# Regrouping the transfers on one DMA queue of a fused attention and MLP kernel

## The chip, the cores and the metric

The kernel runs on one core of a Trainium2 chip. The metric is the device time of one execution in microseconds. Five executions of the kernel before the change took 925.91 to 928.11, with a median of 926.62.

## The reference, cut to what matters

```python
def _attn_ref(q, k, v, g_norm):                 # q, k, v: (8 batches, 8 heads, 576, 64) float32
    kv = np.einsum('bhsd,bhse->bhde', k, v)
    out = np.einsum('bhsd,bhde->bhse', q, kv)
    rms = np.sqrt(np.mean(out * out, axis=-1, keepdims=True) + 1e-06)
    return (out / rms * g_norm)

def _moe_ref(x, w_in, w_out):                   # x: (4608, 512), w_in: (512, 2048), w_out: (2048, 512)
    h = x @ w_in
    sp = np.maximum(h, 0.0) + np.log1p(np.exp(-np.abs(h)))
    g = h * erf(sp)
    return g @ w_out

x = attn_out.transpose(0, 2, 1, 3).reshape(4608, 512)    # the bridge between the two
```

Attention is linear, so each head needs k^T v (64 x 64), q times that, and a normalisation. Its result feeds an MLP whose two weight matrices come as float64. The kernel reads them as pairs of 32-bit words and converts them itself.

## The kernel before the change

**Groups and periods.** The 4608 tokens are worked on in nine groups of 512: one for the first 512 tokens of each batch, and a ninth made of the last 64 tokens of all eight. While one group goes through the MLP, the attention of the next one is computed beside it, two heads (a pair) at a time, four pairs to a group. The hidden features are handled in 16 tiles of 128.

- Head (L729 to L758): the attention of group 0, and the first loads.
- First loop (L822 to L928), groups 0 and 1, one hidden tile in each step n. In group 0 the weights are loaded (load_w, L208) and converted to float32 (w_split, w_join). In group 1 each tile is cut into three parts (w_upper L645 on ACT, w_lower L661 on DVE), so that a product of full precision can be made from three fast ones, and the parts are stored to a scratch area in HBM (L668, L672). ACT cuts into a buffer of four in the pool w_in_p, and has to wait until the store of the tile that had that buffer before has landed.
- Second loop (L976 to L1077), groups 2 to 8. I call one pass a **period** and number it by its m, 8 to 36. In period m PE makes four hidden tiles (hidden, L676: 12 products at L634 each, which read x_forms and w_in_parts), and after them the four results of the period before (result, L950: again 12 products at L634 each, which read g_forms and w_out_parts). In between stand the few matmuls of one attention pair of the next group (visit L428, mean L483).

**What a period loads.** Four tiles of w_in and four of w_out, 768 KB each, come back from the scratch area through load_parts (L765, issued at L773). w_in has four buffers: one comes free when its hidden tile is done, and is needed again at the same place a period later. w_out has seven: all four of a period come free only when PE is through with the last of the four results, since every result reads all four. Three tiles are thus loaded ahead, and the fourth follows in the first buffer that comes free. A period also loads k, v and q of the pair that is two ahead (load_pair L123, load_q L152): k and v as 115 rows of five tokens (L141) and one odd row (L146) each, q in eight small transfers of 32 and 40 KB that bring it in 32 x 32 blocks (L162), which DVE then turns (turn, L314, at L318). k, v and q have two buffers each. At the end of a group (periods 8, 12, 16 and so on) four output tiles are stored (store, L698, at L705).

**What sets the order.** Every engine runs the order in which the program is written. All these transfers are issued by SP, one after the other, so a transfer that has to wait holds up all that are behind it. A transfer also waits for a semaphore: the program gives the transfers of this queue eight semaphores in turn, so one can be issued only when the one that stands eight places ahead of it has landed. That is why the trace shows SP waiting at L162 for "DMA v_sb".

In a period, the calls fetch(place) set the order, with place 0 to 3 after the four hidden tiles and 4 to 7 after the four results, and `loads` stands at place 3:

```python
    FETCH = ("", "in", "in", "out", "in", "out", "in", "out out")
    load_parts("out", BATCH)
```

So SP sees, from one period to the next: w_in, w_in, k, v, q (8 transfers), w_out, w_in, w_out, w_in, w_out, w_out, with the output stores among the last ones. In the steps of groups 0 and 1, k, v and q of a pair are loaded in one go, in the step that has a pair's first products (`loads` after visit).

Of the kernel before, what the change touches and what calls it, by code (L numbers as in the profile page):

```python
# [49 lines left out]

BATCH = 4
LAG = 5


FIRST = 2
WHOLE = 2
SHIFT = 4096.0
SQ = 32
# [3 lines left out]
def kernel(  # L62
# [10 lines left out]
    nc = tc.nc  # L73
    P = 128
    B, H, S, D = q.shape
# [4 lines left out]
    NP = H // 2  # L80
# [30 lines left out]
    exp_ln_table()  # L111


    q_sb, k_sb, v_sb = {}, {}, {}


    q_last = early.tile([P, 2, 2, D], FP32, name="q_last", bufs=1)
# [1 line left out]
    def chunks(T):  # L119

        return 6 if T == 0 else 5

    def load_pair(i, turned=True):  # L123
        T, p = divmod(i, NP)
        if T >= B:
            return
        pool = early if i in (2, 3) else kvp
        side = nc.scalar if i < 3 else nc.sync
        if T == 0:
            t = pool.tile([P, G if pool is early else S], FP32, name="q_sb", tag="q")  # L130
            t = q_sb[T, p] = t[:, 0:G].rearrange("p (j h d) -> p j h d", j=J, h=2)
            nc.sync.dma_start(
                out=t, in_=q[T, 2 * p : 2 * p + 2, 0:G, :].rearrange("h (p j) d -> p j h d", j=J)
            )
        for name, got, src in (("k", k_sb, k), ("v", v_sb, v)):
            C = chunks(T)
            rows, rest = divmod(S, C)
            assert rest < 2
            t = got[T, p] = pool.tile([rows + rest, 2, C, D], FP32, name=f"{name}_sb", tag=name)
            heads = src[T, 2 * p : 2 * p + 2]  # L140
            side.dma_start(  # L141
                out=t[:rows].rearrange("r h c d -> r h (c d)"),
                in_=heads[:, : S - rest].rearrange("h (r c) d -> r h (c d)", c=C),
            )
            if rest:
                side.dma_start(  # L146
                    out=t[rows:, :, 0], in_=heads[:, S - rest :].rearrange("h r d -> r h d")
                )
        if T > 0 and turned:
            load_q(i)  # L150

    def load_q(i):  # L152


        T, p = divmod(i, NP)
        t = q_sb[T, p] = kvp.tile([P, S], FP32, name="q_sb", tag="q")
        for n in range(P // SQ):
            h, w = divmod(n, D // SQ)
            to = t[n * SQ : n * SQ + SQ].rearrange("a (j b) -> a j b", b=SQ)
            for head, js in ((1 - h, slice(0, G // 2 // SQ)), (h, slice(G // 2 // SQ, S // SQ))):  # L160
                src = q[T, 2 * p + head, :, w * SQ : w * SQ + SQ]
                nc.sync.dma_start(  # L162
                    out=to[:, js], in_=src.rearrange("(j a) b -> a j b", a=SQ)[:, js]
                )
# [78 lines left out]
    def w_join(which, f, k):  # L243
# [122 lines left out]
    def attention(T, p, pools=None, in_parts=False):  # L366
# [5 lines left out]
        apart = FIRST < T < B  # L372
# [177 lines left out]
            split_lower()  # L550

        def loads():
            load_pair(T * NP + p + 2)

        if T == 0:
            return products, apply, halve, mean, norm
# [4 lines left out]
        first_ = (partial(prepare, T, p),) if (T, p) == (1, 0) else ()  # L561
        then_ = partial(turn, *then)
        if apart:
            pieces = (first_, (visit, halve, keep_tail), (loads, then_))
            return (*(partial(chain, *group) for group in pieces), mean, norm, *after)
        pieces = (first_, (visit, loads), (halve, keep_tail) if halves else (keep_tail,))
        return (*(partial(chain, *group) for group in pieces), mean, partial(chain, norm, then_), *after)
# [176 lines left out]
    for i in range(NP + 3):  # L744
        for piece, p in ((0, i), (1, i - 1), (4, i - 3), (3, i - 2)):
            if 0 <= p < NP:
                first[p][piece]()
        if i == 1:
            for _ in range(RAW - 2):
                w_next("load")  # L750
            load_pair(NP, turned=False)
            load_pair(NP + 1, turned=False)
        for what in w_rounds.get(i, ()):
            w_next(what)


    w_late.append(True)
    load_q(NP)  # L758
    first_batch, batches = FIRST * NB, NG * NB
    w_seq = {  # L760
        which: [(which, f) for _ in range(NG - FIRST) for f in range(FC)] for which in ("in", "out")
    }
    w_seq["out"][:0] = [("out", f) for f in range(FC - BATCH, FC)]

    def load_parts(which, n):  # L765


        pool = w_out_p if which == "out" and len(w_seq["out"]) > BATCH else w_in_p
        for _ in range(n):
            if w_seq[which]:  # L770
                key = w_seq[which].pop(0)
                t = pool.tile([P, 3, G], FP32, name=f"w_{which}_parts", tag="w")
                nc.sync.dma_start(out=t, in_=w_kept[key])  # L773
                w_now.setdefault(key, []).append(t)
# [47 lines left out]
    for n in range(FIRST * FC + 1):  # L822
        T, f = divmod(n, FC)
        if n == FC:
# [4 lines left out]
            w_in_p = ctx.enter_context(tc.tile_pool(name="w_in_p", bufs=BATCH))  # L829
# [17 lines left out]
        while due(0):  # L847
            weights()
        done = n - LAG + 1
        if T == 0 and done >= 0:  # L850
# [11 lines left out]
        elif T < FIRST:  # L862
# [10 lines left out]
            for i, c in blocks:  # L873
# [4 lines left out]
                    start=(c == 0),  # L878
                    stop=(c == KC - 1),
                )  # L880
        if T < FIRST:
            if n == whole:
                old_h = acc.tile([P, BATCH, G], FP32, name="h", tag="e")
            h = hs[n] = old_h[:, n - whole] if n >= whole else unit("h_sb")
            s = ss[n] = unit("s_sb")
            if n in plain:
                nc.scalar.copy(h, plain.pop(n))
            else:
                nc.scalar.activation(h, n_ps, AF.Copy, scale=SHIFT - 1.0)
# [12 lines left out]
            nc.scalar.activation(s, h, AF.Softplus)  # L902
            if n == 0:
                w_next("split")
            if n == 1:
                load_q(NP + 1)
            for piece in steps[f][1]:
                piece()
            if f % BATCH == BATCH - 1:
                for i in range(n - BATCH + 1, n + 1):  # L910
                    nc.scalar.activation(ss[i], ss[i], AF.Erf)  # L911
                softplus_table()
            if T == FIRST - 1:
# [10 lines left out]
        if T < FIRST:  # L924
            for piece in steps[f][2]:
                piece()
    for n in range(whole, FIRST * FC):
        gates(n)  # L928

# [3 lines left out]
    ctx.enter_context(tc.tile_pool(name="shift_r", bufs=1, side="right")).tile([P, 496], FP32, name="shift_r")  # L933
    late_r = ctx.enter_context(tc.tile_pool(name="late_r", bufs=1, side="right"))
    gate_r = ctx.enter_context(tc.tile_pool(name="gate_r", bufs=1, side="right"))
    w_out_p = ctx.enter_context(tc.tile_pool(name="w_out_p", bufs=7, side="right"))

    def part(h, half):
        return h[:, :, half * 2 * P : half * 2 * P + 2 * P]
# [30 lines left out]
                store(T, j, es[j], cols)  # L970


    FETCH = ("", "in", "in", "out", "in", "out", "in", "out out")
    load_parts("out", BATCH)
    g_next = []
    for m in range(first_batch, batches + 1):  # L976
        T, b = divmod(m, NB)
        todo = []
        last_ = b == NB - 1 and T + 1 < NG
        if T + 1 < NG:  # L980
            todo = list(attention(T + 1, b, in_parts=last_))
            if b == 0:
                side = late_r if T % 2 == FIRST % 2 else late
# [3 lines left out]
        def piece():  # L987
            if todo:
                todo.pop(0)()
# [13 lines left out]
                todo.pop(0)()  # L1003

        def fetch(place):
            for which in FETCH[place].split():
                load_parts(which, 1)


# [40 lines left out]
        for j in range(J):  # L1050
# [60 lines left out]
```

## Time and profile before the change

| | us |
|---|---|
| median of five executions | 926.62 |
| the profiled execution | 925.91 |
| its span, first to last instruction | 924.1 |
| PE busy | 899.4 |
| DVE busy | 750.7 |
| ACT busy | 589.1 |
| start of period 8 (first period) | 249.86 |
| start of period 9 | 274.36 |
| start of period 10 | 299.54 |
| start of period 27 | 709.26 |

The page splits the span into 40 slices; PE's busy share is full in nearly all of them, except at the two ends. SP's queue (q1) moved 256.74 MB, and its packets took 75.7% of what the 16 DMA engines had.

How to read the views: the page's groups give a line of the kernel, the engine, what it writes and reads, the number of instructions, their busy time and mean, and after the second bar the idle time ahead of them and what ended it. The chain of waits gives start, duration and the piece of work, followed back from the last instruction (here for one stretch of time); a DMA in it lasts from its issue until it has landed; "SPq L162" is SP issuing at that line. A table of windows gives for each stretch its length, then busy time and number of instructions of PE, PE's weight loads, DVE, ACT and POOL, then the granted TensorE clock, the share of DMA time and GB/s. SP's timeline gives start, duration, and what was issued, with equal issues merged.

### The profile page before, as it was taken

Reading aid. Unit: us, or ns where it says so; the run is one execution under the profiler, and the core shown is the slowest. Engines: PE = TensorE matmul, PEld = TensorE weight load, DVE = VectorE, ACT = ScalarE, POOL = GpSimd, SP = SyncE. Lnnn points to the kernel's source line nnn. Section 1 sums busy time; section 2 is a strip of 40 time slices with the busy share of each in tenths; the row PEclk is TensorE's granted clock in tenths of the full one; section 3 lists DMA queues with packets and bytes.
Section 4 is the critical chain, followed back from the end, with each engine's and each line's share of the span. In section 5 each row is a group of like instructions: output and inputs, shape, how many; then the busy total and the mean of one; then the engine's idle time right before and its main releaser. Section 6 shows DMA issues by size and latency. Waiting matters only on the chain.

```text
span 924.1 us, 13591 instructions
## 1 busy us (share of the span) xinstructions
PE 899.4 (97%) x4990; PEld 668.9 (72%) x4990; DVE 750.7 (81%) x1088; ACT 589.1 (64%) x783; POOL 2.4 (0%) x10
## 2 busy tenths in 40 slices
PE   5999999989999999999999999999999999999998
PEld 4444445655587888788888788878887888888886
DVE  2799958878588889888888888888888888886777
ACT  3878666767675666656666666666666766665552
POOL 1000000000000000000000000000000000000000
PEclk9999999999999999999999999999999999999999
DMA  9877507698688888988898888887889788778871
GB/s 254 239 213 254 153 1 273 241 368 323 225 297 304 310 315 306 347 310 313 311 339 309 309 313 314 296 311 290 292 310 387 274 301 311 291 284 315 327 269 50
DMA packets 143210, 259.91 MB, mean 281 GB/s; under 512 B 78936, under 2 KB 101800, under 8 KB 143144
## 3 DMA queue, kind: packets, MB, share of 16 engines
q1 hardware_dynamic: 141432, 256.74, 75.7%
q10 hardware_dynamic: 1648, 2.29, 0.8%
q8 instruction: 40, 0.66, 0.3%
q14 instruction: 26, 0.21, 0.1%
q0 software_dynamic: 64, 0.00, 0.0%
HBM read 224.40 MB, written 34.60 MB: 280 GB/s over the span
## 4 chain that ended last, share of the span: by engine, by line
PE 76%; DMA 14%; ACT 3%; DVE 3%; SPq 1%; issue 1%; DVEq 0%; ACTq 0%
PE n_ps L634 42%; PE m_ps L634 21%; DMA w_out_parts<-w_out 5%; PE o_ps L690 5%; PE h_ps L874 4%; DMA v_sb<-in_v_dram 3%; DMA w_in_parts<-w_in 2%; DMA w_in<-w_new 2%; PE at_ps L449 1%; PE at_ps L435 1%; ACT s_sb L911 1%; DMA w_raw<-in_moe_w_out_dram 1%; DMA q_sb<-in_q_dram 1%; DMA q_last<-in_q_dram 1%; PE at_ps L497 1%
## 5 line engine op out<-in xcount | busy, mean ns | idle before, releaser
L634 PE MATMUL n_ps<-w_out_parts,g_forms 128*128 128x512 f32 x928 | 232.0, 391 | 2.0 <-DMA w_out_parts<-w_out 1.9
L634 PE MATMUL n_ps<-x_forms,w_in_parts 128*128 128x512 f32 x896 | 225.0, 393 | 1.6 <-DMA w_in_parts<-w_in 1.2
L634 PEld LDWEIGHTS n_ps<-w_out_parts,g_forms 128*128 128x128 f32 x928 | 172.2, 188 | 39.7 <-DMA w_out_parts<-w_out 4.9
L634 PEld LDWEIGHTS n_ps<-x_forms,w_in_parts 128*128 128x128 f32 x896 | 166.2, 188 | 39.0 <-ACT h L1024 1.4
L1039 ACT ACTIVATE s<-h 128x512 f32<-128x512 f32 x112 | 70.9, 633 | 180.8 <-DVE h L612 180.8
L612 DVE TENSOR_TENSOR h<-m_ps,h 128x512 f32<-128x512 f32 x116 | 79.9, 689 | 61.4 <-ACT h L1024 39.7
L634 PE MATMUL m_ps<-w_out_parts,g_forms 128*128 128x512 f32 (+1 forms) x468 | 124.4, 388 | 0.0
L634 PE MATMUL m_ps<-x_forms,w_in_parts 128*128 128x512 f32 x448 | 119.8, 389 | 0.0
L690 PE MATMUL o_ps<-w_out_sb,h_sb 128*128 128x512 f32 x224 | 101.5, 596 | 0.2 <-DVE h_sb L820 0.2
L634 PEld LDWEIGHTS m_ps<-w_out_parts,g_forms 128*128 128x128 f32 x468 | 87.5, 188 | 18.5
L634 PEld LDWEIGHTS m_ps<-x_forms,w_in_parts 128*128 128x128 f32 x448 | 84.1, 188 | 17.5
L612 DVE TENSOR_TENSOR e<-m_ps,e 128x512 f32<-128x512 f32 (+1 forms) x117 | 80.3, 687 | 13.7 <-PE m_ps L634 2.4
L1024 ACT ACTIVATE h<-n_ps 128x512 f32<-128x512 f32 x112 | 65.4, 584 | 16.1 <-PE n_ps L634 16.1
L690 PEld LDWEIGHTS o_ps<-w_out_sb,h_sb 128*128 128x128 f32 x224 | 41.4, 190 | 45.2 <-issue 42.8
L578 DVE SCALAR_TENSOR_TENSOR g_forms<-g_forms 128x1024 fp32r<-128x1024 f32 x58 | 71.1, 1225 | 2.0
L575 DVE TENSOR_TENSOR g_forms<-h,g_forms 128x1024 fp32r<-128x1024 f32 x58 | 70.6, 1217 | 1.2 <-ACT g_forms L572 1.1
L572 ACT ACTIVATE g_forms<-h 128x1024 fp32r<-128x1024 f32 x58 | 58.9, 1051 | 15.1 <-PE m_ps L634 11.0
L1071 DVE TENSOR_TENSOR h<-h,s 128x1024 f32<-128x1024 f32 x56 | 65.9, 1217 | 0.0
L874 PE MATMUL h_ps<-xT,w_in_sb 128*128 128x512 f32 x144 | 64.6, 595 | 0.0
L607 DVE SCALAR_TENSOR_TENSOR e<-n_ps,e 128x512 f32<-128x512 f32 x88 | 60.1, 683 | 1.7 <-PE n_ps L634 1.7
L109 ACT ACT_TABLE_LOAD x44 | 56.5, 1283 | 0.7
L874 PEld LDWEIGHTS h_ps<-xT,w_in_sb 128*128 128x128 f32 x144 | 27.1, 190 | 33.4 <-issue 31.5
(119 smaller groups left out, 990.6 us busy)
## 6 DMA issues: line engine op xcount, KB each, us to landing
w_out_parts<-w_out SPq DMA_DIRECT2D x116, 768.0 KB
w_in_parts<-w_in SPq DMA_DIRECT2D x112, 768.0 KB
w_in<-w_new SPq DMA_DIRECT2D x16, 768.0 KB
w_raw<-in_moe_w_in_dram SPq DMA_DIRECT2D x16, 512.0 KB
w_raw<-in_moe_w_out_dram SPq DMA_DIRECT2D x8, 1024.0 KB
out_dram<-e SPq DMA_DIRECT2D x32, 256.0 KB
k_sb<-in_k_dram SPq DMA_DIRECT2D x28, 287.5 KB
v_sb<-in_v_dram SPq DMA_DIRECT2D x28, 287.5 KB
```

The lines of the kernel that those rows point to most:

```text
L109: nc.scalar.preload_act_table_set("softplus")
L572: nc.scalar.activation(high, x, AF.Copy, scale=1.0 + 2.0**-13)
L575: nc.vector.tensor_tensor(out=low, in0=x, in1=high.bitcast(FP32), op=ALU.subtract)
L578: nc.vector.scalar_tensor_tensor(out=both, in0=low.bitcast(FP32), scalar=SHIFT, in1=high.bitcast(FP32), op0=ALU.mult, op1=ALU.add,)
L607: nc.vector.scalar_tensor_tensor(out=out_, in0=ps, scalar=scale, in1=out_, op0=ALU.mult, op1=ALU.add)
L612: nc.vector.tensor_tensor(out=out_, in0=ps, in1=out_, op=ALU.add)
L634: nc.tensor.matmul(ps[:, cols], lhsT=weights(form, k), rhs=moving(form, k)[:, cols], start=(form == forms[0] and k == 0), stop=(form == fo ...
L690: nc.tensor.matmul(o_ps[j], lhsT=g[:, j * P : j * P + P], rhs=w_out_sb[:, f, :], start=(f == 0), stop=last,)
L874: nc.tensor.matmul(plain[i], lhsT=w_in_sb[:, i % FC, c], rhs=xT[T][:, c, :], start=(c == 0), stop=(c == KC - 1),)
L1024: nc.scalar.activation(h[:, i], n_ps, AF.Copy, scale=SHIFT - 1.0)
L1039: nc.scalar.activation(s[:, i], h[:, i], AF.Softplus)
L1071: nc.vector.tensor_tensor(out=part(h, half), in0=part(h, half), in1=part(s, half), op=ALU.mult)
```

## The change

Only the order of SP's transfers, and the moment at which they are written into it, is changed. The instructions of PE, DVE, ACT and POOL keep their order.

- In periods, `loads` moves from the third place to the first (ahead of the period's first hidden tile), w_in's four tiles follow one after the other at places 1 to 4, and w_out's four tiles follow at place 7, ahead of the output store of the last result. SP so sees: k, v, q (8), w_in x 4, w_out x 4, and in a group's last period three stores ahead of w_out's four and one behind them.
- Ahead of the first period seven tiles of w_out are loaded, not four. At the end only the very last tile of w_out goes into a buffer of w_in, not the last four.
- In groups 0 and 1 the transfers of q, and from the third pair of group 1 on also those of k and v, are put on a list (to_fetch) and issued a few at a time: two after each load of weights in the head, four at the end of each step of the first loop. In the steps with stores, the first stores now come directly after k and v, and the q's follow in fours.

```diff
+OUT_BUFS = 7
...
-    def load_pair(i, turned=True):
+    def load_pair(i, later=False):
...
-            side.dma_start(
-                out=t[:rows].rearrange("r h c d -> r h (c d)"),
-                in_=heads[:, : S - rest].rearrange("h (r c) d -> r h (c d)", c=C),
-            )
+            due_ = [
+                partial(
+                    side.dma_start,
+                    out=t[:rows].rearrange("r h c d -> r h (c d)"),
+                    in_=heads[:, : S - rest].rearrange("h (r c) d -> r h (c d)", c=C),
+                )
+            ]
             if rest:
...
+            if later:
+                to_fetch.extend(due_)
+            else:
+                for start in due_:
+                    start()
-        if T > 0 and turned:
+        if T > 0:
             load_q(i)
+            if T > FIRST and not later:
+                fetch_some(P)
...
-                nc.sync.dma_start(
-                    out=to[:, js], in_=src.rearrange("(j a) b -> a j b", a=SQ)[:, js]
+                to_fetch.append(
+                    partial(
+                        nc.sync.dma_start,
+                        out=to[:, js],
+                        in_=src.rearrange("(j a) b -> a j b", a=SQ)[:, js],
+                    )
                 )
+
+    def fetch_some(n):
+        for due_ in to_fetch[:n]:
+            due_()
+        del to_fetch[:n]
...
         def loads():
-            load_pair(T * NP + p + 2)
+            load_pair(T * NP + p + 2, later=not apart)
...
         if apart:
-            pieces = (first_, (visit, halve, keep_tail), (loads, then_))
+            pieces = ((loads,), (visit, halve, keep_tail), (then_,))
...
-            load_pair(NP, turned=False)
-            load_pair(NP + 1, turned=False)
+            load_pair(NP)
+            load_pair(NP + 1)
         for what in w_rounds.get(i, ()):
             w_next(what)
+            if what == "load":
+                fetch_some(2)
...
-    load_q(NP)
...
-        pool = w_out_p if which == "out" and len(w_seq["out"]) > BATCH else w_in_p
+        pool = w_out_p if which == "out" and len(w_seq["out"]) > 1 else w_in_p
...
-            if n == 1:
-                load_q(NP + 1)
...
             for piece in steps[f][2]:
                 piece()
+            fetch_some(4)
...
-    w_out_p = ctx.enter_context(tc.tile_pool(name="w_out_p", bufs=7, side="right"))
+    w_out_p = ctx.enter_context(tc.tile_pool(name="w_out_p", bufs=OUT_BUFS, side="right"))
...
-    FETCH = ("", "in", "in", "out", "in", "out", "in", "out out")
-    load_parts("out", BATCH)
+    FETCH = ("", "in", "in", "in", "in", "", "", "out out out out")
+    FETCH_LAST = ("", "in", "in", "in", "in out", "", "", "")
+    fetch_some(P)
+    load_parts("out", OUT_BUFS)
...
-            for which in FETCH[place].split():
+            for which in (FETCH_LAST if m >= batches - 1 else FETCH)[place].split():
```

More of the change, by code (lines that the diff above doesn't have):

```diff
@@ L111 @@
     exp_ln_table()
-    q_sb, k_sb, v_sb = {}, {}, {}
+    q_sb, k_sb, v_sb, to_fetch = {}, {}, {}, []
     q_last = early.tile([P, 2, 2, D], FP32, name="q_last", bufs=1)
@@ L140, in load_pair @@
             heads = src[T, 2 * p : 2 * p + 2]
-            side.dma_start(
-                out=t[:rows].rearrange("r h c d -> r h (c d)"),
-                in_=heads[:, : S - rest].rearrange("h (r c) d -> r h (c d)", c=C),
-            )
-            if rest:
-                side.dma_start(
-                    out=t[rows:, :, 0], in_=heads[:, S - rest :].rearrange("h r d -> r h d")
-                )
-        if T > 0 and turned:
+            due_ = [
[5 more added lines that the diff above has]
+            ]
+            if rest:
+                due_.append(
+                    partial(
+                        side.dma_start,
+                        out=t[rows:, :, 0],
+                        in_=heads[:, S - rest :].rearrange("h r d -> r h d"),
+                    )
+                )
+            if later:
[4 more added lines that the diff above has]
+        if T > 0:
             load_q(i)
+            if T > FIRST and not later:
+                fetch_some(P)
     def load_q(i):
@@ L161, in load_q @@
                 src = q[T, 2 * p + head, :, w * SQ : w * SQ + SQ]
-                nc.sync.dma_start(
-                    out=to[:, js], in_=src.rearrange("(j a) b -> a j b", a=SQ)[:, js]
-                )
+                to_fetch.append(
+                    partial(
+                        nc.sync.dma_start,
+                        out=to[:, js],
+                        in_=src.rearrange("(j a) b -> a j b", a=SQ)[:, js],
+                    )
+                )
+    def fetch_some(n):
+        for due_ in to_fetch[:n]:
+            due_()
+        del to_fetch[:n]
     def load_last(p):
```

## The prediction

> **What bounds the kernel now.** I read the page first (engine shares, costliest groups), then where matrix work starts late, then the chain of waits in the first groups, then the SP queue's timeline with the trace's semaphore steps, which tell when a transfer has landed.
>
> ```profile
> span 924.1 us, 13591 instructions
> ...
> PE 899.4 (97%) x4990; PEld 668.9 (72%) x4990; DVE 750.7 (81%) x1088; ACT 589.1 (64%) x783; POOL 2.4 (0%) x10
> ...
> L634 PE MATMUL n_ps<-w_out_parts,g_forms 128*128 128x512 f32 x928 | 232.0, 391 | 2.0 <-DMA w_out_parts<-w_out 1.9
> ...
> L634 PEld LDWEIGHTS n_ps<-w_out_parts,g_forms 128*128 128x128 f32 x928 | 172.2, 188 | 39.7 <-DMA w_out_parts<-w_out 4.9
> ```
>
> PE is busy 97% of the span, and its instructions keep their order in the changed program (so do DVE's, ACT's and POOL's; only SP's order changes). So the change can only take away, or add, time in which PE starts late. I took the start of each period from PE's timeline (first L634 product that reads w_in_parts): 249.86, 274.36, 299.54, ... An undisturbed period with attention in it lasts 23.81. From 249.86 to 709.26 there are 19 such periods; their excess over 23.81 sums to 7.05 us, about what PE's waits for weight tiles come to (1.9 and 4.9 above, and 1.2 for w_in_parts). That is all the periods can give back. The other losses lie ahead of them:
>
> ```profile
> 173.98 8.18 DMA v_sb<-in_v_dram
> 182.16 0.02 issue
> 182.18 0.31 SPq L162
> ...
> 182.53 0.45 SPq L162
> ...
> 183.59 4.74 DMA w_in<-w_new
> ...
> 188.41 0.63 ACT w_new L596
> ...
> 194.99 0.49 ACT h_sb L889
> 195.49 0.04 issue
> 195.53 3.32 PE n_ps L634 x8
> ```
>
> This is the chain of waits in group 1. SP cannot issue the seventh q transfer (L162) until v has landed; behind the eight q's stand the stores of cut weights (L672); ACT's L596 needs the stored buffers; ACT's L889 behind it frees PE's bank. PE stands 3.39 us. It is then slow for a while, too:
>
> ```profile
> 192.00:195.00 3.00, 0.14 (x1) 0.00 (x0) 0.00 (x0) 2.98 (x6) 0.00 (x0) 1.00 1.01 397
> 195.00:200.00 5.00, 4.47 (x12) 3.32 (x12) 4.87 (x8) 3.78 (x7) 0.00 (x0) 0.66 0.91 374
> 224.00:229.00 5.00, 3.57 (x21) 2.51 (x22) 3.79 (x6) 3.80 (x7) 0.00 (x0) 1.00 1.04 419
> ```
>
> The column after the engines is the granted clock: 0.66 after the gap, and ten products start 0.20 later each than their usual 0.23, so 2.0 us more. The same chain ends at 225.65 with a gap of 1.43 (loss 1.59), and the clock stays at 1.00.
>
> **The first groups.** (1) Around 42 to 48 us DVE's transpose (L318) waits 2.56 us for the first turned q, whose eight transfers start at 36.18, behind two waits of SP for w_raw buffers. The change puts four of them ahead of those waits, and the last two land right behind the w_out tile of 35.76 (44.02) instead of at 45.96. PE's late start at 46.97 (0.75 over its usual step) goes: **-0.75**. (2) At 176 the two stores now stand directly behind v' (the odd row of v). Their data is ready at 176.64 and 177.97 (DVE's L602), so they wait for no q. They queue behind v, which lands at 182.16, and then need 1.87 each (the landings' spacing in a run of such tiles): 184.0 and 185.9 instead of 186.39 and 188.33. ACT is free at 184.80, so its L596 ends 2.4 us sooner and PE's gap falls from 3.55 to about 1.1: **-2.45**. A gap under 1.43 kept the full clock: **-2.0**. What is late next is ACT itself, with tables and Erf. (3) At 216 the same with less: the queue is fuller now (the stores between two v's need 8 x 1.87 + 9 x 0.64, k and v 4.9, q 1.5, together 27.1 against PE's 26.9 for four steps), so I take 1.2 of the 1.59: **-1.2**. Sum: **-6.4**, bounds 0 (stores not earlier) and -7.3 (all of 0.75 + 3.55 + 2.0 + 1.59, less 0.6 that ACT needs anyway). The q's in fours add no transfer; a pair's twelve are issued within three steps, and its turn (L318) comes five later.
>
> **The periods.** Here the queue decides:
>
> ```profile
> 353.33 0.33 SPq L141 DMA_DIRECT2D k_sb<-in_k_dram  x1
> 353.70 1.07 SPq L146 DMA_DIRECT2D k_sb<-in_k_dram  x1
> 354.82 0.77 SPq L141 DMA_DIRECT2D v_sb<-in_v_dram  x1
> 355.63 4.64 SPq L146 DMA_DIRECT2D v_sb<-in_v_dram  x1
> 360.37 8.51 SPq L162 DMA_DIRECT2D q_sb<-in_q_dram  x8
> 368.92 0.46 SPq L773 DMA_DIRECT2D w_out_parts<-w_out  x1
> ```
>
> Eight transfers are in flight at most: each takes one of eight semaphores in turn. So q7 waits for v, q8 for v', and the first weight tile goes out only then; call that moment W (here 368.92). That tile lands at W + 4.45 (373.40; also 349.46 after 345.02), the next ones 1.86 apart, then k and v 2.45 each: they take five of the sixteen engines (the semaphore rises by five steps, and 1280-byte packets run five at a time in 90 of the 149 us in which any runs). From W to W there are 23.38 us on average over twelve periods (22.59 to 24.78), and 26.34 over the five with output stores. Three of the one and one of the other need 96.5, PE 95.2: **the queue is the slower of the two**, and PE's waits are its deficit.
>
> The change leaves the transfers and that dead time (v landed, q8, W, 4.45 less 1.86) as they are, once a period: so the same 17 loops, 412.2 us from W = 272.01 to 684.21. What it moves is which tile comes first after W. Before, a period's weights alternate and PE meets its last one late; now w_in's four come first after W and w_out's four before k, and the first product of the next period needs the first w_in. So a period can start at W + 4.45 at the earliest.
>
> Step by step, on the old clock: period 8 starts at 249.86, the first w_out goes out at 252.77 (as now: DVE's L820 frees the room). Seven instead of four w_out, and no w_in among them: 7 tiles against 4 + 2, +1.86, so W = 272.01 + 1.86 = 273.9. w_in lands at 278.35, where period 9 would start at 274.36: PE waits **4.0**. W again 26.3 later, w_in at 304.6, period 10 due at 302.2: **+2.3**, less what a slow clock behind the first wait has used up. From there the deficit of each store loop, about 1.2, is waited for like now. Period 26 starts at 273.9 + 412.2 + 4.45 = 690.5, period 27 at 714.3 instead of 709.26: **+5.05**. Bounds: -7.05 (every wait gone) to +12 (twelve loops 0.5 longer as well). I take 5.05, the measured loops being the nearest rows. Nothing is dear elsewhere: w_out's tile for the next results lands 4 to 8 us after the period's start and is needed at 15 (288.01 - 274.36 + 1.4); k, v and q have most of a period. Behind the four w_out, which wait for PE's last product, stand on SP the store of j = 3, which nobody waits for, and k, v and q, which still have that period. After 709 a period's eight tiles take 15 of 22.24 us: nothing.
>
> A page would say otherwise. The Trainium skill, "DMA: Bandwidth & Descriptors", Specifications, gives about 358 GB/s of HBM to a core; the estimate from it is 20.0 us for a period's 7.18 MB, so the queue would soon catch up and the sum would be some 7 us in favour. The measured loops decide against it.
>
> **Sum.** -6.4 + 5.05 = -1.35, the span from 924.1 to 922.75. The profiled execution took 925.91 (1.8 around its span), 0.7 under the median 926.62; on the median I forecast **925.3**.
>
> **Rivals.** *A, as worked out:* 925.3, itself 921 to 928. *B, the loops run at their fast end* (22.6 to 23.0, as four of the twelve do, because four tiles of one kind stand together): PE waits 4.0 and 2.2 once and never again; 19 x 23.81 + 6.2 = 458.6 instead of 459.4, -0.8, with -6.4: 919.4. For it: the spread of the loops; against: its cause, an engine that lags by up to 2.4 us late in a run of tiles, isn't touched. *C, slower: the loops run at their slow end*, 23.9 instead of 23.38. That decides from 23.81 on, PE's own period: beyond it nothing is caught up between two stores, and twelve times 0.52 come on top: +6.2, 931.5. For it: three of the twelve are there now, and the change makes the w_out block wait for PE; against: the block before it is still in the queue for 5 us then. *D, the first groups gain nothing*, because SP, held at the fourth q of a four until the first store has landed, issues the later stores no sooner: 931.7. Against: the first two stores stand ahead of that q.
>
> **Chances.** A 0.50, B 0.25, C 0.16, D 0.09. A measurement tells 0.2% (1.9 us) from no change. A lies across that bound: 0.20 faster, 0.27 within, 0.03 slower. Faster 0.45, same 0.27, slower 0.28. The range 917 to 932.5 takes in B and, barely, C and D.
>
> **What would show it.** Right: no PE gap near 190 above 1.5 us and clock 1.00 there; period 8 starting near 243.5; PE waiting for w_in_parts about 4 us at period 9 and 2 at period 10, each at the period's first product; hardly any wait for w_out_parts; W to W still 23.4 and 26.3. Wrong: period starts that do not follow W + 4.45, loops of another length, or waits for k, v or q.

## The result, and the profile after

The changed kernel took 931.89 us in the median (22 executions, 929.42 to 940.69) where the kernel before took 927.31 (43 executions on the same chips): a ratio of 1.0050, 95% interval 1.0037 to 1.0064, so 4.6 us slower. The forecast was 925.3. The profiled execution took 929.02, 3.1 more than the profiled one of before (925.91), and was its kernel's fastest execution.

The page of the changed kernel; after the second bar stands the idle time ahead of PE's products and what ended most of it:

```profile
span 927.2 us, 13656 instructions
...
PE 900.0 (97%) x4990; PEld 670.6 (72%) x4990; DVE 750.9 (81%) x1088; ACT 590.6 (64%) x783; POOL 2.4 (0%) x10
...
L658 PE MATMUL n_ps<-x_forms,w_in_parts 128*128 128x512 f32 x896 | 226.7, 396 | 9.5 <-DVE x_forms L602 3.9
L658 PE MATMUL n_ps<-w_out_parts,g_forms 128*128 128x512 f32 x928 | 230.4, 391 | 0.0
```

L658 is before's L634. PE's work is the same; the waiting has moved from w_out's products (2.0 us before, now none) to w_in's (9.5). The 3.9 put down to DVE is period 9's first product at 273.72: DVE's x_forms had long been done, and by the semaphore steps of the trace the first w_in tile, issued at 269.39, landed at 273.58.

The stretches that answer the prediction's marks (same columns as before, clock behind the engines):

```profile
189.00:192.00 3.00, 2.87 (x7) 0.95 (x5) 1.66 (x3) 2.98 (x5) 0.00 (x0) 1.00 1.00 388
192.00:197.00 5.00, 4.25 (x65) 3.27 (x65) 4.66 (x8) 3.63 (x8) 0.00 (x0) 1.00 0.97 350
218.50:223.50 5.00, 3.70 (x14) 2.25 (x13) 3.42 (x6) 4.42 (x8) 0.00 (x0) 1.00 0.95 329
...
275.00:280.00 5.00, 5.00 (x17) 3.98 (x16) 1.74 (x2) 1.23 (x2) 0.00 (x0) 0.67 0.97 319
...
303.00:308.00 5.00, 5.00 (x18) 4.00 (x17) 3.48 (x4) 1.48 (x3) 0.00 (x0) 0.74 1.01 420
```

In group 1 the full clock stays behind the first gap, as forecast. The second gap (218.5 to 223.5) is still there. In the periods two slow stretches are new: 0.67 behind period 9's wait, 0.74 behind period 10's (before, the clock was 1.00 behind the starts of both).

One regular period of SP's queue (start, duration, what was issued):

```profile
417.29 2.21 SPq L798 DMA_DIRECT2D w_in_parts<-w_in  x4
421.60 1.83 SPq L798 DMA_DIRECT2D w_out_parts<-w_out  x4
423.48 2.87 SPq L161 DMA_DIRECT2D k_sb<-in_k_dram  x2
426.40 5.97 SPq L161 DMA_DIRECT2D v_sb<-in_v_dram  x2
432.47 8.41 SPq L187 DMA_DIRECT2D q_sb<-in_q_dram  x8
440.98 2.23 SPq L798 DMA_DIRECT2D w_in_parts<-w_in  x4
```

W to W (417.29 to 440.98) is 23.69. By the semaphore steps the last w_out landed at 436.03; W came 4.95 behind it, and the first w_in landed 4.44 behind W. From one big tile to the next across a pair's k, v and q there are 9.15 us on average over 17 periods (8.99 before); inside a run of tiles the median is 1.85. I call it **the step over the pair**; much of what follows is about it.

### The profile page after: what moved, and what is told of

It is laid out like the page before. It is cut to its first block, busy times and chain, and to the rows that moved or that the text cites. A ratio compares the mean times of both kernels' runs of the same rounds, so it can differ in the third digit from the quotient of the medians.

```text
span 927.2 us, 13656 instructions
## 1 busy us (share of the span) xinstructions
PE 900.0 (97%) x4990; PEld 670.6 (72%) x4990; DVE 750.9 (81%) x1088; ACT 590.6 (64%) x783; POOL 2.4 (0%) x10
## 4 chain that ended last, share of the span: by engine, by line
PE 72%; DMA 13%; DVE 7%; ACT 4%; issue 2%; SPq 1%; DVEq 0%; ACTq 0%
PE n_ps L658 39%; PE m_ps L658 19%; PE o_ps L714 5%; PE h_ps L899 5%; DMA out_dram<-e 2%; DMA w_in_parts<-w_in 2%; DMA v_sb<-in_v_dram 2%; DMA w_in<-w_new 1%; PE at_ps L473 1%; PE at_ps L459 1%; DMA w_out_parts<-w_out 1%; DMA k_sb<-in_k_dram 1%; DMA w_raw<-in_moe_w_in_dram 1%; DMA w_raw<-in_moe_w_out_dram 1%; DVE h L1097 1%
## 5 line engine op out<-in xcount | busy, mean ns | idle before, releaser
L658 PE MATMUL n_ps<-x_forms,w_in_parts 128*128 128x512 f32 x896 | 226.7, 396 | 9.5 <-DVE x_forms L602 3.9
L658 PE MATMUL n_ps<-w_out_parts,g_forms 128*128 128x512 f32 x928 | 230.4, 391 | 0.0
L658 PEld LDWEIGHTS n_ps<-x_forms,w_in_parts 128*128 128x128 f32 x896 | 167.3, 189 | 47.4 <-DVE x_forms L602 4.3
L658 PEld LDWEIGHTS n_ps<-w_out_parts,g_forms 128*128 128x128 f32 x928 | 172.8, 188 | 35.6 <-DMA w_out_parts<-w_out 0.3
L658 PE MATMUL m_ps<-w_out_parts,g_forms 128*128 128x512 f32 (+1 forms) x468 | 124.3, 388 | 0.0
L658 PE MATMUL m_ps<-x_forms,w_in_parts 128*128 128x512 f32 x448 | 121.3, 393 | 0.0
L658 PEld LDWEIGHTS m_ps<-w_out_parts,g_forms 128*128 128x128 f32 x468 | 87.5, 188 | 18.4
L658 PEld LDWEIGHTS m_ps<-x_forms,w_in_parts 128*128 128x128 f32 x448 | 85.3, 190 | 17.9
```

Of the source, the lines that this page charges most:

```text
L658: nc.tensor.matmul(ps[:, cols], lhsT=weights(form, k), rhs=moving(form, k)[:, cols], start=(form == forms[0] and k == 0), stop=(form == fo ...
```

## The experiments

In the expectations T and R with a number name the rival theories. The kernel before ran beside each batch, at medians of 927.0 to 930.3, so compare ratios. "Periods 8 to 27" is the time between the starts of these two in the profile: 459.40 before, 467.05 after.

### The two parts apart

With the first groups' part alone, the periods are those of before:

```diff
-            pieces = ((loads,), (visit, halve, keep_tail), (then_,))
+            pieces = (first_, (visit, halve, keep_tail), (loads, then_))
...
-    FETCH = ("", "in", "in", "in", "in", "", "", "out out out out")
...
+    FETCH = ("", "in", "in", "out", "in", "out", "in", "out out")
...
-    load_parts("out", OUT_BUFS)
+    load_parts("out", BATCH)
...
```

> Only the first groups' part of the change (q, k and v in twos and fours); the periods' order is that of before, four tiles of w_out ahead. T1 (the change is a sum of two parts, each paid where it is made): period 8 starts at about 245.4 as in the changed kernel, periods 8 to 27 take about 459.4 as before, so 4.5 us less than before: 922.8 against a median of 927.3, ratio 0.995. R1 (the periods' queue is bound by an absolute rate, so that an earlier start of period 8 is waited away in the periods): 0 to 1 us less than before, periods 8 to 27 take some 463.

Measured: 921.67, ratio 0.9942 (0.9923 to 0.9961). Period 8 starts at 245.16, periods 8 to 27 take 460.02. T1 holds.

The converse takes the kernel before and puts in only the change's `pieces`, FETCH, FETCH_LAST and seven tiles ahead.

> Only the periods' part of the change (k, v, q, then w_in's four, then w_out's four; seven tiles of w_out ahead); the first groups are those of before, with the 3.4 us gap of PE near 192. T1: period 8 starts at 249.9, W of period 8 comes 24.0 after it, period 9 waits about 4, and periods 8 to 27 take 467 instead of 459.4: 7.6 us more than before in the profile, up to 9 in the medians (changed kernel +4.6 plus the 4.5 that the first groups gave): 935 to 936, ratio 1.008 to 1.010. R1 (the waits come from PE arriving earlier than the queue): only 3 to 4 us more than before.

Measured: 937.06, 1.0104 (1.0080 to 1.0128); 468.59 for the periods. R1 falls. The parts add up: -0.58% and +1.04% against +0.50%. So both signs of the forecast were right, and the sizes were not.

### What stands ahead of the first w_in

```diff
-    load_parts("out", OUT_BUFS)
+    load_parts("out", BATCH)
```

(and w_out's last four tiles at places 1 to 4 of FETCH_LAST)

> The changed kernel, but with four tiles of w_out ahead of the first period instead of seven (the last period's four go in w_in's buffers, as before). T1 (the queue's phase: a period starts at W + 4.45, and three tiles fewer ahead bring W forward by 3 x 1.86 = 5.6): W of period 8 comes 18.4 after its start, period 9 does not wait, period 10 waits about 2.5, and period 27 starts 4 to 6 us earlier than in the changed kernel: 926 to 928 against 931.9, ratio to before about 0.999 to 1.001. R2 (a slow clock behind each wait is the larger part): 6 to 8 us less, since the wait at period 9 goes with its 1.5 us of slow products: 924 to 926. R3 (what stands ahead does not matter, the block of w_out behind PE's last product sets W in every period): no change to the changed kernel.

Measured: 927.12, 1.0002 (0.9983 to 1.0021), 0.48% or 4.4 us under the changed kernel: T1's size, less than R2's; R3 falls. Its profiled execution (935.13) lay 8 us over its median and isn't read for times; in it the first w_in lands at 271.06, ahead of period 9's start at 272.45, as T1 has it.

Then, still with four tiles ahead, k, v and q went behind w_in's four, so that w_out stands behind the pause:

```diff
-            pieces = ((loads,), (visit, halve, keep_tail), (then_,))
-            return (*(partial(chain, *group) for group in pieces), mean, norm, *after)
+            def mean_(table=True):
+                loads()
+                mean(table)
+            pieces = ((visit, halve, keep_tail), (then_,))
+            return (lambda: None, *(partial(chain, *group) for group in pieces), mean_, norm, *after)
```

> The changed kernel with four tiles of w_out ahead and k, v and q of a pair issued behind w_in's four instead of ahead of them. T1 (what hurts is that w_in, which PE needs first in a period, stands directly behind the dead time of k, v and q): now w_out stands behind it, which PE needs 15 us later, so period 9 and 10 do not wait, and 24 us of room against a deficit of about 10 over the 17 loops are enough: periods 8 to 27 take 453 to 455, 918 to 921. R5 (a loop takes 23.4 and 26.9 in whatever order, and the room is used up because w_out is only issued at the period's end): waits move to w_out at 15 us into a period, 926 to 928, as with four ahead alone.

Measured: 929.63, 1.0006 (0.9987 to 1.0025): R5. PE's waits in the periods, by who ended them (total, times, longest), in an execution of 933.36:

```profile
PE n_ps L661 <- DMA w_out_parts<-w_out: 9.9, 10, 1.7
```

No wait for w_in is left, but w_out now waits, at group ends above all, where SP stands 25.9 us in all for the data of output stores with w_out's tiles behind them.

Putting the store of j = 3 ahead of w_out's tiles (fetch(BATCH + j) below the store's lines) was to explain the longer loops with stores:

> The changed kernel with the fourth output store of a group (j = 3) ahead of w_out's four tiles instead of behind them; nothing else. It tests why the loops with stores took 26.86 here and 26.34 before. T7 (the order around the store, with the queue standing still while SP waits for it, makes the 0.5): five loops 0.5 us shorter, 929 to 930 against 931.9. R7 (waiting for the store's data holds w_out's four back by about 1.5 us in each of five group ends): 933 to 939. R8 (the 0.5 is the queue's own scatter): within 0.7 us of the changed kernel.

Measured: 932.47, 1.0037 (1.0018 to 1.0056), and the five loops with stores average 26.96 (26.87 in the changed kernel, 26.33 before). The order around that store is not the cause. In the run of the periods' part alone the five average 27.08; in the first-groups run, with before's order, 26.50 (25.75 to 27.62). So the half microsecond goes with the changed order (26.87, 26.96, 27.08 against 26.33, 26.50). It lies between the weight tiles: the seven steps up to a tile's landing, behind the first tile, sum to 15.1 to 15.5 us with the changed order and to 14.4 and 14.8 with before's. What makes them longer stays open.

### Why a loop takes 23.4

The forecast rested on loops of 23.38 and 26.34. Two causes were in the trace: k and v use five of the sixteen engines, and q7, q8 and the first tile wait for v in the round of eight semaphores. First try, k and v as 96 rows of six tokens (`chunks` returns 6 always):

> The changed kernel, with k and v loaded as 96 rows of six tokens for all pairs instead of 115 rows of five and an odd row (the sums over tokens are the same; 24 small products of a pair in place of 20, some 0.2 us more of PE per pair). T1 (k and v cost 2.45 us each because five of sixteen engines carry them, and the odd rows' two transfers hold two of the eight semaphores): k and v land under 1 us apart each, W to W falls from 23.4 to about 20 and from 26.9 to about 23.5, the queue gets ahead of PE's 23.8, PE waits for w_in once (about 4 us or less at period 9) and hardly again: 7 to 10 us less than the changed kernel, 922 to 925. R4 (the loops are bound by bytes, whatever engines carry them): W to W stays at 23.4 and the time rises by some 3 us for the added products: 935.

Measured: 1021.64, 1.1016 (1.0987 to 1.1046). Neither theory saw this. The products of k and v (L473) in one period, first of the changed kernel, then of this run (count, min/median/max ns, first and last start):

```profile
L473 PE MATMUL at_ps<-v_sb,k_sb x40: 217/218/267, 356.7 to 357.3; 64*64 64x64 f32 x20, 51*64 51x64 f32 x16, 52*64 52x64 f32 x4
```

```profile
L473 PE MATMUL at_ps<-v_sb,k_sb x48: 217/265/361, 361.3 to 364.4; 64*64 64x64 f32 x24, 32*64 32x64 f32 x24
```

40 products start within 0.6 us, 15 ns apart; in halves of 64 and 32 rows 48 take 3.1 us, 65 ns apart. The granted clock drops as well, to 0.74 from 365 to 370; over the whole execution its mean is 0.957, in the changed kernel 0.996.

The Trainium skill, "TensorEngine Tiling (Array Packing)", Key Properties, says that a change of the tiling mode drains TensorE; products that alternate between 64 and 32 rows fit that, and this is a cause from a page, not one that I took apart. The queue itself did part of what was hoped: W came 1.8 to 2.8 us behind the last w_out, 2.3 on average (the 1.4 in an expectation below is the distance from k's landing), and the step over the pair is 7.1 us. But with PE slowed, the time says nothing on the loops.

So the rows were cut by sixteens and the tiles and products left alone:

```diff
+            cuts = (0, rows) if T == 0 else (0, 112, rows)
-                    out=t[:rows].rearrange("r h c d -> r h (c d)"),
...
+                    out=t[lo:hi].rearrange("r h c d -> r h (c d)"),
...
+                for lo, hi in zip(cuts, cuts[1:])
```

> The changed kernel, but k and v of groups 1 and up are loaded as 112 rows and 3 rows (and the odd row) in place of 115 rows and the odd row; the tiles, PE's products and all orders stay as they are. In the run with 96 rows a transfer of k or v took 0.4 to 1.2 us of the queue instead of 2.45 and the first w_in went out 1.4 us behind the last w_out's landing instead of 5.2. T1 (the five-engine transfers are the queue's deficit): W to W falls from 23.4 to some 20.5, period 9 waits 4.3 - 3.3 = 1 us and no later period waits; periods 8 to 27 take 453 to 455 instead of 467; the gaps at 193 (1.03) and 221 (1.46) shrink too: 916 to 919 against 931.9. R4 (the queue is bound by bytes): loops stay at 23.4, time within 1 us of the changed kernel. R6 (the two added transfers per pair take two more of the eight semaphores and SP's 0.4 us each): 2 to 4 us more than the changed kernel.

> The version with the first groups' part alone (921.7) and k and v as 112 + 3 rows as in the run beside it. T1: the loops no longer exceed PE's period, so the 7.6 us that periods 8 to 27 take over 19 x 23.81 go, and 1 to 2.5 us of the first groups: 911.5 to 914. R4: 921 to 922. R6: 923 to 926.

Measured: 928.35, 0.9984 (0.9966 to 1.0002), and with the first groups' part alone 920.69, 0.9904 (0.9877 to 0.9931). By the ratios that is 6.1 and 3.5 us better than without the split: far from T1's 13 to 16 us and 8 to 10, more than R4's 1, and not R6's loss. By the loops R4 holds: they take 23.48, and 26.46 with stores. The profiled executions show only 1.7 and 1.3 of the gain, and in the periods (466.61 and 458.08) 0.4 and 1.9. SP's queue in the changed kernel with the split:

```profile
347.15 1.74 SPq L801 DMA_DIRECT2D w_out_parts<-w_out  x4
348.95 1.43 SPq L164 DMA_DIRECT2D k_sb<-in_k_dram  x3
351.41 4.58 SPq L164 DMA_DIRECT2D v_sb<-in_v_dram  x3
357.28 6.79 SPq L190 DMA_DIRECT2D q_sb<-in_q_dram  x8
364.19 2.29 SPq L801 DMA_DIRECT2D w_in_parts<-w_in  x4
```

v landed at 362.04, 1.4 behind the last w_out (360.68) instead of 3.7 on average. But q2 to q8 could only be issued once that w_out had landed, some 0.5 us from one to the next, so W came at 364.19 all the same, 3.5 behind. The step over the pair is 8.51 instead of 9.15.

Next, q ahead of k and v in the periods (load_q and fetch_some(P) moved above the loop over k and v):

> The changed kernel, but in the periods q's eight transfers are issued ahead of k and v. In the changed kernel W comes 4.65 us behind the landing of the last w_out: k and v land 3.7 behind it, and q7 and q8 wait for v. With 112 rows k and v landed 1.3 behind it, but seven q's at 0.45 each still had to be issued then (3.9). Now q5 to q8 wait for w_out's four, k and v for q1 to q4, and the first w_in for q5 only. T9 (the dead time is made by the order in which the eight semaphores come round): W comes about 1 us behind the last w_out, the first w_in queues behind k and v without a pause, loops fall to 20 to 21, period 9 waits under 1 and the periods need some 455 instead of 467: 919 to 921. R10 (the engines owe the bytes all the same: whatever is saved behind the last w_out comes back between the tiles, as in the run with 112 rows, 14.3 to 15.0): loops stay above 23, 928 to 932.

> The first groups' part alone, with the old order of the weights, and q ahead of k and v in the periods. T9: the 7.6 us of the periods' waits go: 913 to 915. R10: 920 to 922 as with the first groups' part alone.

> As the run beside it, and k and v in 112 + 3 rows. T9: nothing left to gain in the periods, the first groups lose the gap at 221 (1.4) and widen that at 193 (0.7): 912 to 915. R10: 919 to 921, as with the split alone.

Measured: 949.93, 1.0213 (1.0185 to 1.0242); 941.69, 1.0122 (1.0099 to 1.0145); 919.26, 0.9887 (0.9863 to 0.9911). T9 fails in all three; R10 missed the size in the first two, and its 919 to 921 came true in the third. W does come sooner (2.7 behind the last w_out instead of 4.7), but k and v are now issued only as the q's land, and come 3.2 to 4.2 apart; the step over the pair grows to 10.7. With the split beside it (third run) it is 9.15 and does no harm.

Last, q on a queue of its own, which leaves twelve transfers a period to SP's eight semaphores:

```diff
-                        nc.sync.dma_start,
+                        (nc.gpsimd if T > FIRST else nc.sync).dma_start,
```

> The changed kernel, but in the periods q's eight transfers are issued by POOL on a queue of its own; SP's queue has k, v, w_in's four and w_out's four left, twelve transfers in place of twenty. T11 (the dead time is the queue running empty: eight semaphores, of which twelve small transfers in a row hold all, so that the first w_in is only issued when v has landed, 4.65 behind the last w_out, and lands 4.45 later): now the first w_in waits for the first w_out only and is queued long before, it follows v at the usual spacing; a loop takes eight tiles (16.4 with the scatter seen) and k and v (4.9), 21 to 21.5; period 9 waits 0 to 1, later ones not: 917 to 921 against 931.9. R10 (the engines owe the bytes whatever the order): loops 23 and up, 929 to 933. R12 (POOL's queue gets in the way: its transfers are slower to start and share the engines): 933 or more, with waits for q.

> The first groups' part alone with the old order of weights (921.7), and q on POOL's queue in the periods. T11: the 7.6 us of waits in the periods go: 913 to 915. R10: 921 to 922. R12: more than 922.

> As the run beside it, with k and v as 112 + 3 rows. T11: the periods have nothing left to give, the first groups give 0.7: 912 to 915. R10: 919 to 921, as with the split alone. R12: more than 921.

Measured: 939.58, 1.0107 (1.0091 to 1.0122); 934.71, 1.0068 (1.0056 to 1.0080); 920.28, 0.9913 (0.9900 to 0.9926). In the first of them (an execution of 943.43, 3.9 over its median) SP's queue no longer runs empty:

```profile
352.98 1.97 SPq L798 DMA_DIRECT2D w_out_parts<-w_out  x4
355.00 2.11 SPq L161 DMA_DIRECT2D k_sb<-in_k_dram  x2
357.27 5.49 SPq L161 DMA_DIRECT2D v_sb<-in_v_dram  x2
362.86 4.69 SPq L798 DMA_DIRECT2D w_in_parts<-w_in  x4
```

The first w_in is issued 4.3 us before the last w_out lands (367.17). And yet it lands at 377.23, ten behind it. The semaphore steps tell why. Of w_in's sixteen, eleven came from 369.87 to 370.53, four from 372.36 to 373.19, and one at 377.23; k's five came from 366.49 to 367.14 and at 370.51, v's from 369.91 to 370.58 and at 374.21. So the engines that carried k and v come late to w_in, and one of the five, already 1.9 to 2.7 behind its neighbours in the w_out tiles, comes last by far. These five are the bound now, and where PE waits it is the one late step. PE's waits for weight tiles in the second run's periods are:

```profile
PE n_ps L658 <- DMA w_in_parts<-w_in: 8.0, 10, 1.6
PE n_ps L658 <- DMA w_out_parts<-w_out: 3.4, 4, 1.4
```

Each of the fourteen is shorter than the time by which the sixteenth step of its tile came behind the fifteenth: had the fifteenth been the last, none would be left. That lag is 3.1 us in the median of the periods' weight tiles in the first run and 4.9 in the second, and 0.5 or less in every other run here, the third of these too. So it comes with q on POOL's queue and k and v on five engines together; why, no run shows. With the split as well (third run), PE's waits in the periods are:

```profile
PE at_ps L523 <- DVE bd_kv L368: 2.1, 3, 0.9
```

No weight tile is waited for any more. So there are two limits side by side, the semaphores' round and the engines that carry k and v, and each alone holds the loop: T11 was half of the cause, and R10, by which the order changes nothing, falls with this run's step over the pair of 4.48. R12's times came true in the first two runs, but not its waits for q, of which there is none. In time the third run only reaches R10's 919 to 921, for what it gains in the periods (455.72 against 458.38 with q ahead and the split) it loses ahead of them (0.9) and behind them (1.5): period 27 takes 25.01 instead of 23.75, with a wait for DVE's x_last. The last pair of runs puts both remedies on the changed kernel, to see what its own order costs then:

> The changed kernel with both of the queue's limits taken away together: k and v as 112 + 3 rows and q on POOL's queue in the periods; seven tiles of w_out ahead as in the change. On the old order both together took periods 8 to 27 to 455.7, where either alone gave 458.1 and 471.4. T13 (two limits in parallel, the semaphores' dead time and the five engines, either of which holds a loop at 23.4): periods 9's wait for w_in stays, 2 to 4 us since W of period 8 still comes behind seven tiles, with some slow clock behind it; after that no wait for a weight tile: periods 8 to 27 take 455 to 459 instead of 467, 919 to 923. R13 (what helped on the old order was its alternation of w_in and w_out): waits for w_in at each group's end remain, 463 to 467, 927 to 932.

> As the run beside it, but four tiles of w_out ahead. T13: W of period 8 comes 5.6 earlier, period 9 does not wait, the periods take 453 to 455, what is left are waits for DVE: 917 to 920. R13: 922 to 927.

Measured: 921.81, 0.9916 (0.9894 to 0.9937), and 921.52, 0.9910 (0.9887 to 0.9933). T13 holds for the first: 458.12 for the periods, of which period 9 waits 2.5 for w_in, and after it no wait for a tile:

```profile
PE at_ps L523 <- DVE bd_kv L368: 2.4, 4, 1.0
PE n_ps L661 <- DVE e L634: 1.7, 1, 1.7
PE at_ps L523 <- DVE x_last L484: 1.7, 1, 1.7
```

(The line with DVE e is period 9, where w_in landed at 270.95 and PE started at 271.09.) The second missed T13's 917 to 920: its periods take 458.45 instead of 453 to 455, and it still waits for w_out in five places:

```profile
PE n_ps L661 <- DMA w_out_parts<-w_out: 4.0, 5, 1.3
```

The two remedies, by the profiled executions (step over the pair / periods 8 to 27):

| | neither | 112 + 3 rows | q on POOL | both |
|---|---|---|---|---|
| changed order | 9.15 / 467.05 | 8.51 / 466.61 | 9.85 / 476.50 | 4.19 / 458.12 |
| before's order, first groups' part | 8.98 / 460.02 | 8.46 / 458.08 | 9.11 / 471.41 | 4.48 / 455.72 |

The second row is the one to read as a lesson, for its executions lie within 0.5 us of their medians (in the first row, "neither" is 2.9 under its own and "q on POOL" 3.9 over): alone the remedies give -1.9 and +11.4, the latter by the one late step above, together -4.3. In the median times both together (0.9913) are no faster than the split alone (0.9904).

The best versions lie at ratios of 0.9887 to 0.9916 with overlapping intervals; all have the first groups' part and the split.

## Why the prediction was wrong, point by point

| step | forecast | profile |
|---|---|---|
| (1) first turned q | -0.75 | -0.27 (PE's lead ahead of the store chain) |
| (2) PE's gap near 195 | -2.45 | -2.51 |
| (2) slow clock behind it, and (3) gap near 225 | -2.0 and -1.2 | -1.74 (about 1.6 and 0.15) |
| first groups | -6.4 | -4.51 (245.35 against 249.86) |
| W of period 8 after its start | 24.0 | 24.04 |
| a period's start after W | 4.45 | 4.33, 4.49, 4.52, 4.53 (periods 9, 10, 18, 26) |
| period 9's wait | 4.0 | 4.05 |
| 17 loops from there | 412.2 | 414.58 |
| periods 8 to 27 | +5.05 | +7.65 |

**Right were the mechanisms.** w_in stands behind the pause, and a period that waits starts at W + 4.45: 4.3 to 4.5 at the five waits of the changed kernel, 4.2 to 5.3 at the six of the periods' part alone, and with three tiles fewer ahead 4.4 us of the time come back. The gap near 195 fell from 3.39 to 0.87 us and its slow clock went, though it gave 1.6 us and not 2.0.

**Wrong was step (3).** It took the store chain of group 1's second pair for the one that ends last, and it was no longer. ACT and DVE there, in the kernel before:

```profile
213.78 4.67 DMA w_in<-w_new
218.53 0.63 ACT w_new L596
219.16 0.52 ACT s_sb L902
...
216.05 0.65 DVE L612 TENSOR_TENSOR h_sb<-m_ps,h_sb 128x512 f32<-128x512 f32 x1
```

and in the changed kernel (what ACT waited for in brackets):

```profile
213.57 0.63 ACT L620 ACTIVATE w_new<-w_in_sb 128x512 fp32r<-128x512 f32 x1 [0.74 <-DMA w_in<-w_new]
214.53 0.63 ACT L927 ACTIVATE s_sb<-h_sb 128x512 f32<-128x512 f32 x1 [0.33 <-DVE h_sb L636]
...
213.85 0.65 DVE L636 TENSOR_TENSOR h_sb<-m_ps,h_sb 128x512 f32<-128x512 f32 x1
```

Before, h_sb was done 2.5 us before ACT came to it; now ACT waits for it last. PE had gained 4.4 us on its clock by then, DVE only 2.2 (h_sb at 213.85 instead of 216.05). So PE's gap fell only from 1.43 to 1.30. The store was not early enough either: it landed at 213.49 instead of 218.44, 0.6 sooner on PE's clock and not 1.2, and ACT was done with it 0.33 before DVE; without DVE about 0.5 of the 1.2 would have come. In the two runs with the split alone the gap near 221 is gone altogether and the one near 193 grew from 0.9 to 1.5 and 1.6; that the shorter k and v do this is shown, by which link is not.

**Wrong was "the same 17 loops, 412.2 us".** The twelve regular loops took 23.35 (forecast 23.38), but the five with stores 26.87 instead of 26.34, and the first of them, behind period 8, 27.42. That is 2.4 of the 2.6 that the periods' sum is off; it comes with the changed order in all three executions read for it, from what stays open. PE cannot make it up: its own period is 23.81, and period 10's wait of 1.92 started the slow clock again, which the forecast left out (products 0.2 later each; period 10 took 25.52). In PE's time everything is lost in periods 8 to 10: their excess over 23.81 is 10.0 us against 2.2 before, and that of the other sixteen is 4.6 against 4.8.

**Of the rivals** the slow C (931.5) and D (931.7) came nearest in time, but not by their mechanisms: the regular loops did not slow down, and the first groups gained 4.5. And "an engine that lags isn't touched", said against the fast one, was only half of what the runs showed: the loop is held by the engines that carry k and v and by the semaphores' round at once. The run with both removed brought the step from 9 to 4 us.

The sum: first groups 1.9 short, periods 2.6 too dear, so +3.1 in the profiled executions in place of -1.35. Medians say +4.6; the changed kernel's profiled execution was its fastest.

The Trainium skill, "DMA: Bandwidth & Descriptors", Issuing engines are not separate DMA queues, holds that issuing from more engines saves no more than issue time. With q on POOL alone nothing was gained, as the page has it (step over the pair 9.85 against 9.15); beside the split much was (4.19 against 8.51), since there the transfers that held the round of semaphores were what the queue waited for.

## What to carry to other kernels

A queue with a fixed number of transfers in flight is filled by count and not by bytes: twelve small transfers in a row emptied this one for some 4 us a period, and reordering them only moved the pause. When two limits stand side by side, removing one shows nothing or looks harmful, so test both together before a theory is dropped; and look whether what hurts is still the old limit, or a new one that the remedy itself brought, as the late step here. And when a stall is removed, ask for each later one whether its releaser, measured against the new start of PE, is still the last to arrive.

## What the runs showed of the hardware that I had not expected

- 64 x 64 products over rows in halves of 64 and 51 started 15 ns apart, in halves of 64 and 32 rows 65 ns apart.
- A transfer's cost depends on what stands with it: k to v took 2.46 us on average in SP's order k, v, q (2.3 to 2.9), 3.48 with q ahead (3.2 to 4.2), and 3.76 with q on another queue (3.1 to 4.8).
- With q on POOL's queue and k and v on five engines one of a weight tile's sixteen semaphore steps lags: it came 3.1 and 4.9 us behind the fifteenth in the median of the two runs. With q on SP's queue, or with the split, the median is 0.5 or less (0.27 in the changed kernel, 1.99 at most).
- The length of PE's gap does not alone decide on the granted clock. In the changed kernel it was 0.74 from 303 to 308, behind the gap of 1.92 us at period 10, and 1.00 behind gaps of 0.87, 1.30 and 1.70. In the run with k, v and q behind w_in it was 0.66 over the 5 us behind gaps of 1.36, 1.10 and 0.97 (at 383.5, 482.9 and 580.7) and 1.00 behind one of 1.71 (681.7); with the periods' part alone it stayed at 1.00 behind 2.20 (308.2). So "a gap under 1.43 kept the full clock" in the prediction came true at its place and is no rule.
